# Keeping the feed-forward's steps in traced order on TensorE, in a kernel that adds an S4 convolution and a SiLU feed-forward

## The chip, the cores and the metric

The kernel runs on one core of a Trainium2 chip. The metric is the device time of one execution, in microseconds. A core has five engines with a queue each, which take their instructions in a fixed order: TensorE (PE, matrix products; its weight loads are shown as PEld), VectorE (DVE), ScalarE (ACT), GpSimd (POOL) and SyncE (SP, which here issues DMAs). They wait for each other through semaphores. Products land in PSUM, which the kernel divides into eight banks of 128 x 512 floats; the other operands lie in SBUF.

## The reference

```
xn  = layernorm(x)                       # x = A_u: 1 x 2048 x 576
K   = real(sum_n C * exp(dt*A*l) * dt*B)   # 576 x 2048, from 128 complex modes for each channel
y   = irfft(rfft(xn padded) * rfft(K padded))[:2048] + xn * Dskip
ffn = silu(xn @ w1) @ w2                 # w1: 576 x 4608, w2: 4608 x 576
out = x + y + ffn
```

`B_x` of the inputs is not used. All inputs and the output are float32.

## The kernel before

**Number format.** The large products run on operands split in two parts of a rounded float32 type, a high part `h` and a low part `l` (`h = round(v)`, `l = v - h`: a ScalarE copy and a VectorE subtraction). A product is then three matmuls into the same PSUM bank: h x h, h x l and l x h.

**The feed-forward, `ffn()`.** The 2048 tokens are 16 tiles (`j`) of 128. `half` is the first or second eight of them, `b` a group of four (512 tokens), and `c` one of nine chunks (`NCH`) of 512 of the 4608 hidden units, each of four tiles `t` of 128. A block is `(half, c, b)`: 36 blocks. There are two kinds of step, eight of them for each block:

- `up(blk, t)` (L320 to L342) makes 128 hidden units for 512 tokens: 12 matmuls of 512 columns at L331 (the three part products over four tiles of the contraction) and two at L332 and L333 for the last 64 input channels, all into one bank `ph` (pool `ps1`, two banks). ScalarE then applies the silu (`gf`) and rounds it (`gh`), and VectorE makes `gl`.
- `down(blk, jj)` (L344 to L365) multiplies the block's four `gh`/`gl` pairs with a chunk of w2 for one token tile: for each of two column halves (288 columns) 12 matmuls at L357 into one bank `po` (pool `ps2`, three banks), which VectorE then adds to the accumulator `acc[j]` (L361). In the last chunk of the second half `add_conv` goes ahead of it and adds the convolution's result.

The main loop traces, for block i, first `up` for t = 0 of block i + 1, then the four `down` steps of block i, then `up` for t = 1, 2, 3 of block i + 1; between them it loads and splits the next chunk's weights. The very first block is made ahead of the loop, in half-width pieces (256 tokens, `a` and `e` give the range), so that it can begin with the first two token tiles.

**The side stages, `side()`.** In order: `phase0` (load x, normalize, transpose tiles 0 to 7 into `xh`, `xl`, `x4`; `put_xt`, `put_x4`), the same for tiles 8 to 15 through DRAM (`late`), `natural` (the convolution's parameters), `kgen` (18 rounds, each with 64 small products `kp` at L696 and 8 products `z` at L711), `spread` (products `pu` at L161 and L162), `spectral` (products `pk`, `pu`, `pb` through `mm3`, L826), and `tail`, which with `add_conv` makes the last products `py` (L847). `weave` advances side stages and feed-forward together by given shares of the feed-forward's steps.

**What sets the order.** The Python code traces instructions; a scheduler then lays out each engine's list ahead of the run. It goes by priority, which is the traced order except where `tc.high_priority()` moves an instruction ahead, and it keeps its own account of when operands and buffers come free: where the instruction next in line would wait, another that is ready goes first. `behind(ins)` adds an edge: the instructions in its block stand behind `ins` in the list of their engine. It makes no semaphore wait of its own. `pins` holds instructions to point such edges at; `pins["pe"]` is the last matmul traced so far of an up or down step. Before the change, only two kinds of feed-forward matmuls have such an edge: the half-width ups for t = 2 and 3 of the first block, and in `add_conv` the first product.

Of the kernel before, what the change touches and what calls it, by code (L numbers as in the profile page):

```python
# [26 lines left out]
HD = D // 2  # L27
# [16 lines left out]
def kernel(  # L44
# [21 lines left out]
    nc = tc.nc  # L66
    FT = 4
# [72 lines left out]
    pins = {}  # L140

    def behind(ins):
        return tc.issue_after(ins) if ins is not None else nullcontext()
# [24 lines left out]
    def load_x(j, pool, tag, engines):  # L168

        t = pool.tile([P, 2, D], F32, tag=tag, name=f"{tag}{j}")  # L170
        for i in range(2 if j == 0 else 1):
            for ps, v, eng in quarters(xv, engines):
                if j:
                    eng.dma_start(t[ps], v[:, j:j + 2])
                else:
                    eng.dma_start(t[ps, i], v[:, i])
        pairs[j] = t
        return t[:, 0, :], t[:, 1, :]
# [78 lines left out]
    def ffn():  # L257
        w2v = w2.rearrange("(t p) d -> p t d", p=P)
        blocks = [(half, c, b) for half in range(2) for c in range(NCH) for b in range(2)]
        W1, W2, G = {}, {}, {}  # L260
# [60 lines left out]
        def up(blk, t, a=0, e=512, after=None):  # L321

            half, c, b = blk
            xh, xl, x4 = xts[2 * half + b]
            h1, l1 = W1[half, c, t]
            pool, tag = (ps2, "ps2") if e == 256 and t > 1 else (ps1, "ps1")
            ph = pool.tile([P, 512], F32, tag=tag, name="ph")[:, a:e]
            for n, (w, v) in enumerate(((h1, xh), (h1, xl), (l1, xh))):
                for kt in range(NKT):
                    with behind(after):  # L330
                        nc.tensor.matmul(ph, w[:, kt, :], v[:, kt, a:e], start=n + kt == 0, stop=False)  # L331
            nc.tensor.matmul(ph, h1[:, 4, :], x4[:, a:e], start=False, stop=False)  # L332
            pins["pe"] = nc.tensor.matmul(ph, l1[:, 4, :], x4[:, a:e], start=False, stop=True).ins  # L333
            gf = gp.tile([P, 512], F32, tag="gf", name="gf", bufs=2)[:, a:e]
            if a == 0:
                G[blk, t] = [gp.tile([P, 512], F32R, tag=n, name=n) for n in ("gh", "gl")]
            gh, gl = (g[:, a:e] for g in G[blk, t])
            with tc.high_priority():
                nc.scalar.activation(gf, ph, AF.Silu)  # L339
                pins["gh"] = nc.scalar.copy(gh, gf).ins  # L340
                with behind(pins["w1l2"] if e == 256 else None):
                    pins["gl"] = nc.vector.tensor_sub(gl, gf, gh).ins  # L342

        def down(blk, jj):  # L344
            half, c, b = blk
            j = 8 * half + 4 * b + jj
            js = slice(jj * P, (jj + 1) * P)
            if half == 1 and c == NCH - 1:
                if jj % 2 == 0:
                    add_conv(j, (acc[j], acc[j + 1]))  # L350
            for h in range(2):
                hs = slice(h * HD, (h + 1) * HD)
                po = ps2.tile([P, 512], F32, tag="ps2", name="po")
                n = 0
                for t in range(FT):
                    for g, w in ((0, 0), (0, 1), (1, 0)):
                        pins["pe"] = nc.tensor.matmul(po[:, :HD], G[blk, t][g][:, js], W2[half, c, t][w][:, hs],  # L357
                                                      start=n == 0, stop=n == 3 * FT - 1).ins
                        n += 1
                with tc.high_priority():  # L360
                    nc.vector.tensor_add(acc[j][:, hs], po[:, :HD], acc[j][:, hs])  # L361
            if half == 0 and c == NCH - 1:
                rows = slice(j * P, (j + 1) * P)
                nc.sync.dma_start(dr0[rows, :], acc[j])
                if j % 2:  # L365
                    acc[7 + j], acc[8 + j] = load_x(7 + j, accp, "acc", (nc.sync,))
# [34 lines left out]
        for t in range(FT):  # L401
            if t == 2:
                second = pins["pe"]
            up(blocks[0], t, 0, 256, second if t > 1 else None)
        for t in range(FT):
            up(blocks[0], t, 256, 512)
            yield 3.0

        for i, blk in enumerate(blocks):
            half, c, b = blk  # L410
# [3 lines left out]
            if half == 0 and c == NCH - 1:  # L414
                next_xt(b)

            after = {
                (0, "u0"): [(load_w1, 0)],
                (0, "u1"): [(split_w1, 0), (load_w2, 0), (load_w2, 1)],
                (0, "u2"): [(load_w1, 2)],  # L420
                (1, "u0"): [(split_w1, 2), (split_w2, 0), (load_w2, 2)],
                (1, "d3"): [(split_w2, 1), (load_w2, 3), (split_w2, 2)],
                (1, "u2"): [(split_w2, 3)],
            }
            if new == (1, NCH - 1):

                after = {
                    (0, "u0"): [(load_w1, 0), (load_w2, 0), (load_w2, 1), (load_w1, 2), (load_w2, 2), (load_w2, 3)],
                    (0, "u1"): [(split_w1, 0)],
                    (1, "u0"): [(split_w1, 2), (split_w2, 0)],  # L430
                    (1, "d3"): [(split_w2, 1), (split_w2, 2)],
                    (1, "u2"): [(split_w2, 3)],
                }
            for step in ("u0", "d0", "d1", "d2", "d3", "u1", "u2", "u3"):
                k = int(step[1])
                if step[0] == "d":
                    down(blk, k)
                    yield 3.0
                elif later:
                    up(blocks[i + 1], k)  # L440
                    yield 3.0
                for f, t in after.get((b, step), ()) if more else ():
                    f(*new, t)
                if half == 0 and c == NCH - 1:
                    for kt in {"d3": (0, 1), "u1": (2, 3), "u2": (4,)}.get(step, ()):
                        split_xt(b, kt)
# [391 lines left out]
    def add_conv(j, dsts):  # L838

        py = [pool.tile([P, 512], F32, tag=t, name="py") for pool, t in ((pss, "pss"),) * 3 + ((ps2, "ps2"),)]  # L840
        first = pins["pe"]
        for n in range(16):
            i, q1, q2, h = 1 - n // 8, n // 4 % 2, n // 2 % 2, 1 - n % 2
            o = 64 * q1 + 32 * q2
            rows = slice(64 * h, 64 * h + 64)
            with tc.high_priority() if n else nullcontext(), behind(first):
                mm = nc.tensor.matmul(py[2 * i + h][o:o + 32, :HD], s4[rows], yss[j + i][rows, 2 * q2 + q1],  # L847
                                      start=True, stop=True, tile_position=(64 * h, o), skip_group_check=True)
            if n == 0:
                first = mm.ins  # L850
        for i in range(2):
            del yss[j + i]
            for h in range(2):
                hs = slice(h * HD, (h + 1) * HD)
                nc.vector.tensor_add(dsts[i][:, hs], py[2 * i + h][:, :HD], dsts[i][:, hs])
        for _ in range(2):
            conv_load()
# [165 lines left out]
```

## Time and profile before

| What | us |
|---|---|
| Three runs | 1109.95, 1111.25, 1111.63 |
| Median | 1111.25 |
| Span of the profiled execution, first to last instruction | 1108.2 |
| TensorE matmuls busy | 1102.2 |
| Weight loads busy (beside the matmuls) | 997.5 |
| VectorE busy | 916.6 |
| ScalarE busy | 706.9 |
| GpSimd busy | 72.1 |

The profile has one row for each group of instructions: engine, line of the kernel, operation, what it writes and reads (buffer numbers left out), and how many. In a timeline the two first numbers are the start and the length in microseconds, and brackets give the time for which the engine sat idle ahead of the row and what released it. "Idle" ends when the last semaphore comes. The ends of matmuls are modelled, so that matmuls that follow each other closely overlap in the rows; their starts are recorded. The time of a run is some microseconds longer than the span of the profiled execution, which counts from the first instruction to the last.

The largest groups of DMA are the loads of w1 and w2, 512 and 288 KB each, the spectral stage's operands, and the stores and loads by which the convolution's data change their layout through DRAM.

### The profile page before, as it was taken

To read this page: it belongs to the slowest core of one execution; us is meant where nothing else is said; L and a number is where in the kernel's file an instruction comes from. 1 tells how busy PE (TensorE), PEld (TensorE's weight loads), DVE (VectorE), ACT (ScalarE), POOL (GpSimd) and SP (SyncE) were. 2 spreads that over 40 slices of the span, in tenths; PEclk is the share of its full clock that TensorE was granted. 3 is DMA by queue.
4 is the path that set the end of the run, shared out by engine and by line. 5 is a ranking of instruction groups with operands and counts; after the bars stand their busy time and mean duration, and the time that the engine had idled before them with its cause. 6 is when DMAs were issued, how large, how long until landed. Compare 5 with 4: busy or idle time off the path is not lost.

```text
span 1108.2 us, 22917 instructions
## 1 busy us (share of the span) xinstructions
PE 1102.2 (99%) x9167; PEld 997.5 (90%) x9167; DVE 916.6 (83%) x1543; ACT 706.9 (64%) x1222; POOL 72.1 (7%) x129
## 2 busy tenths in 40 slices
PE   9999999999999999999999999999999999999998
PEld 7989998899998899899999989999999999999887
DVE  7799899999999999999999737787778778784433
ACT  4564466676677676677867536877777878774210
POOL 1100000000000000011000000000000000000111
PEclk9999999999999999999999999999999999999999
DMA  9745512525252525264744173554544455434983
GB/s 270 190 123 160 152 50 61 120 73 131 77 121 83 116 72 118 77 174 154 206 122 103 45 179 109 162 167 123 156 145 152 138 149 170 129 107 127 241 224 87
DMA packets 175755, 148.56 MB, mean 134 GB/s; under 512 B 111088, under 2 KB 142592, under 8 KB 175520
## 3 DMA queue, kind: packets, MB, share of 16 engines
q1 hardware_dynamic: 165328, 112.63, 38.7%
q0 software_dynamic: 9568, 33.62, 9.6%
q8 instruction: 72, 1.18, 0.5%
q10 hardware_dynamic: 752, 0.85, 0.3%
q14 instruction: 35, 0.29, 0.1%
HBM read 102.53 MB, written 44.61 MB: 133 GB/s over the span
## 4 chain that ended last, share of the span: by engine, by line
PE 98%; DMA 1%; DVE 1%; SPq 0%; issue 0%; DVEq 0%
PE po L357 42%; PE ph L331 35%; PE kp L696 3%; PE ph L332 3%; PE ph L333 3%; PE pu L826 2%; PE pb L826 2%; PE pk L826 2%; PE z L711 2%; PE pu L161 1%; PE py L847 1%; DMA acc<-in_A_u_dram 1%; PE pu L162 1%; PE pt L124 0%; DVE w1l L295 0%; PE ptk L490 0%
## 5 line engine op out<-in xcount | busy, mean ns | idle before, releaser
L357 PE MATMUL po<-w2l,gh 128*128 128x288 f32 x1152 | 338.5, 295 | 0.0
L357 PE MATMUL po<-w2h,gl 128*128 128x288 f32 x1152 | 336.4, 295 | 0.0
L357 PE MATMUL po<-w2h,gh 128*128 128x288 f32 x1152 | 336.1, 295 | 0.0
L357 PEld LDWEIGHTS po<-w2h,gh 128*128 128x128 f32 x1152 | 215.2, 188 | 7.7 <-issue 2.8
L357 PEld LDWEIGHTS po<-w2l,gh 128*128 128x128 f32 x1152 | 215.9, 188 | 5.1 <-issue 0.5
L357 PEld LDWEIGHTS po<-w2h,gl 128*128 128x128 f32 x1152 | 215.4, 188 | 0.9
L339 ACT ACTIVATE gf<-ph 128x512 f32<-128x512 f32 (+1 forms) x148 | 86.4, 584 | 143.8 <-PE ph L333 134.8
L331 PE MATMUL ph<-xh,w1l 128*128 128x512 f32 (+1 forms) x592 | 161.3, 385 | 0.0
L331 PE MATMUL ph<-xh,w1h 128*128 128x512 f32 (+1 forms) x592 | 161.3, 387 | 0.0
L331 PE MATMUL ph<-xl,w1h 128*128 128x512 f32 (+1 forms) x592 | 161.1, 385 | 0.0
L361 DVE TENSOR_TENSOR acc<-po,acc 128x288 f32<-128x288 f32 x288 | 126.2, 451 | 37.0 <-PE po L357 35.6
L342 DVE TENSOR_TENSOR gl<-gf,gh 128x512 fp32r<-128x512 f32 (+1 forms) x148 | 99.0, 672 | 64.6 <-ACT gh L340 63.8
L331 PEld LDWEIGHTS ph<-xh,w1l 128*128 128x128 f32 x592 | 108.0, 188 | 20.0
L331 PEld LDWEIGHTS ph<-xl,w1h 128*128 128x128 f32 x592 | 107.9, 188 | 19.8
L331 PEld LDWEIGHTS ph<-xh,w1h 128*128 128x128 f32 x592 | 104.5, 188 | 16.7 <-ACT x L133 0.5
L340 ACT CAST gh<-gf 128x512 fp32r<-128x512 f32 (+1 forms) x148 | 89.5, 608 | 9.5 <-PE po L357 6.6
L653 ACT ACTIVATE c<-th,magic 128x1040 f32<-128x1040 f32 x36 | 42.1, 1168 | 37.9 <-DVE C L676 28.0
L655 ACT ACTIVATE c<-th 128x1040 f32<-128x1040 f32 x36 | 38.7, 1075 | 33.6 <-DVE th L654 33.6
L314 ACT CAST w2h<-w2r 128x576 fp32r<-128x576 f32 x72 | 47.0, 671 | 17.7 <-PE po L357 14.9
L295 DVE TENSOR_TENSOR w1l<-w1r,w1h 128x640 fp32r<-128x640 f32 x72 | 56.9, 817 | 0.2
L332 PE MATMUL ph<-x,w1h 128*128 128x512 f32 (+1 forms) x148 | 57.0, 386 | 0.0
L333 PE MATMUL ph<-x,w1l 128*128 128x512 f32 (+1 forms) x148 | 56.9, 385 | 0.0
(185 smaller groups left out, 1828.8 us busy)
## 6 DMA issues: line engine op xcount, KB each, us to landing
w2r<-in_B_w_dram SPq DMA_DIRECT2D x72, 288.0 KB, 3.8
w1r<-in_B_w_dram SPq DMA_DIRECT2D x35, 512.0 KB, 3.8
d1u<-u POOLq DMA_DIRECT2D x32, 288.0 KB, 2.5
d1k<-stage SPq DMA_DIRECT2D x18, 512.0 KB, 6.8
ur<-d1u SPq DMA_DIRECT2D x32, 288.0 KB, 3.7
kr<-d1k SPq DMA_DIRECT2D x32, 288.0 KB, 2.9
d<-yo POOLq DMA_DIRECT2D x32, 288.0 KB, 4.0
ys<-d SPq DMA_DIRECT2D x32, 288.0 KB, 11.8
```

What stands on the lines that cost most here:

```text
L295: pins["w1l"] = nc.vector.tensor_sub(l1, src, h1).ins
L314: pins["w2h"] = nc.scalar.copy(h2, r2).ins
L331: nc.tensor.matmul(ph, w[:, kt, :], v[:, kt, a:e], start=n + kt == 0, stop=False)
L332: nc.tensor.matmul(ph, h1[:, 4, :], x4[:, a:e], start=False, stop=False)
L333: pins["pe"] = nc.tensor.matmul(ph, l1[:, 4, :], x4[:, a:e], start=False, stop=True).ins
L339: nc.scalar.activation(gf, ph, AF.Silu)
L340: pins["gh"] = nc.scalar.copy(gh, gf).ins
L342: pins["gl"] = nc.vector.tensor_sub(gl, gf, gh).ins
L357: pins["pe"] = nc.tensor.matmul(po[:, :HD], G[blk, t][g][:, js], W2[half, c, t][w][:, hs], start=n == 0, stop=n == 3 * FT - 1).ins
L361: nc.vector.tensor_add(acc[j][:, hs], po[:, :HD], acc[j][:, hs])
L653: nc.scalar.activation(c65, th, AF.Identity, bias=magic)
L826: nc.tensor.matmul(dst, st, mv[:, hs], start=n == 0, stop=n == 3 * len(terms) - 1)
```

## The change

Each matmul of a down step gets an edge to the last feed-forward matmul traced ahead of that half step (`head`). In an up step of full width the twelve matmuls of L331 get one to the last feed-forward matmul traced ahead of the step (`after`). The half-width ups of the first block stay as they were. An instruction of a side stage has no such edge, and may stand between any two matmuls of the feed-forward. Nothing else is edited; lines behind the edits move by 2 or 4.

```
@@ up @@
             h1, l1 = W1[half, c, t]
             pool, tag = (ps2, "ps2") if e == 256 and t > 1 else (ps1, "ps1")
             ph = pool.tile([P, 512], F32, tag=tag, name="ph")[:, a:e]
+            if after is None and a == 0 and e == 512:
+                after = pins["pe"]
             for n, (w, v) in enumerate(((h1, xh), (h1, xl), (l1, xh))):
                 for kt in range(NKT):
                     with behind(after):
@@ down @@
             for h in range(2):
+                head = pins["pe"]
                 hs = slice(h * HD, (h + 1) * HD)
                 po = ps2.tile([P, 512], F32, tag="ps2", name="po")
                 n = 0
                 for t in range(FT):
                     for g, w in ((0, 0), (0, 1), (1, 0)):
-                        pins["pe"] = nc.tensor.matmul(po[:, :HD], G[blk, t][g][:, js], W2[half, c, t][w][:, hs],
-                                                      start=n == 0, stop=n == 3 * FT - 1).ins
+                        with behind(head):
+                            pins["pe"] = nc.tensor.matmul(po[:, :HD], G[blk, t][g][:, js], W2[half, c, t][w][:, hs],
+                                                          start=n == 0, stop=n == 3 * FT - 1).ins
                         n += 1
```

In the old list of TensorE the matmuls of up to three `po` and of one or two `ph` were interleaved; in the new one each `ph` and each `po` is finished before the next begins, with side products in between.

More of the change, by code (lines that the diff above doesn't have):

```diff
@@ L327, in up @@
             ph = pool.tile([P, 512], F32, tag=tag, name="ph")[:, a:e]
+            if after is None and a == 0 and e == 512:
+                after = pins["pe"]
             for n, (w, v) in enumerate(((h1, xh), (h1, xl), (l1, xh))):
@@ L351, in down @@
             for h in range(2):
+                head = pins["pe"]
                 hs = slice(h * HD, (h + 1) * HD)
@@ L356, in down @@
                     for g, w in ((0, 0), (0, 1), (1, 0)):
-                        pins["pe"] = nc.tensor.matmul(po[:, :HD], G[blk, t][g][:, js], W2[half, c, t][w][:, hs],
-                                                      start=n == 0, stop=n == 3 * FT - 1).ins
+                        with behind(head):
+                            pins["pe"] = nc.tensor.matmul(po[:, :HD], G[blk, t][g][:, js], W2[half, c, t][w][:, hs],
+                                                          start=n == 0, stop=n == 3 * FT - 1).ins
                         n += 1
```

## The prediction

> **What bounds the kernel now.** I read the page's totals first, then the chain of waits, then the timelines of the first 50 us, then the busy time by stage.
>
> ```profile
> span 1108.2 us, 22917 instructions
> PE 1102.2 (99%) x9167; PEld 997.5 (90%) x9167; DVE 916.6 (83%) x1543; ACT 706.9 (64%) x1222; POOL 72.1 (7%) x129
> PEclk9999999999999999999999999999999999999999
> PE 98%; DMA 1%; DVE 1%; SPq 0%; issue 0%; DVEq 0%
> ```
>
> TensorE is 99% of the span and 98% of the chain. Matmul ends are modelled, so "busy" alone could hide waits; the distance between starts can't. From the chain in order of time, and from a timeline in the middle of the kernel:
>
> ```profile
> 71.45 3.86 PE ph L331 x17
> 101.01 4.78 PE po L357 x36
> ...
> 301.19 0.62 PE L331 MATMUL ph<-xh,w1h 128*128 128x512 f32 x2
> 301.65 0.29 PE L357 MATMUL po<-w2h,gh 128*128 128x288 f32 x1
> ...
> 303.10 0.29 PE L357 MATMUL po<-w2h,gl 128*128 128x288 f32 x1
> 303.23 0.40 PE L331 MATMUL ph<-xh,w1h 128*128 128x512 f32 x1
> ```
>
> An up matmul (512 columns, L331) takes 3.86/17 = 0.227 us from start to start, a down matmul (288 columns, L357) 4.78/36 = 0.133 us. Going from up to down costs nothing (301.65 - 301.19 = 0.46 us for two ups), nor from down to up (303.23 - 303.10 = 0.13 us). TensorE is a full pipe, and the order in which the feed-forward's matmuls fill it has no price of its own. A new order can only lose, by making the pipe wait for an operand or a buffer, unless there are waits to win back. VectorE is the next candidate:
>
> ```profile
> 17.00:40.82 23.82, 23.67 (x189) 23.47 (x189) 21.89 (x59) 13.96 (x29) 3.87 (x4) 1.00 0.84 243
> 40.82:167.00 126.18, 126.18 (x740) 113.45 (x738) 113.95 (x192) 71.80 (x102) 4.81 (x5) 1.00 0.48 125
> 167.00:636.00 469.00, 469.00 (x4973) 423.32 (x4975) 451.84 (x677) 323.98 (x487) 21.52 (x39) 1.00 0.41 109
> 636.00:1050.00 414.00, 414.00 (x2727) 381.63 (x2716) 294.00 (x536) 281.55 (x578) 28.76 (x53) 1.00 0.53 149
> ```
>
> (Columns: stretch, length, then PE, PEld, DVE, ACT, POOL busy.) While the convolution kernel is built (167 to 636 us) VectorE is busy 451.84 of 469 us, so only 17.2 us are free; after 636 it has 29% free. Before 41 us, while x and the weights are being prepared, it is busy 92% too.
>
> **The change, part by part.** No matmul, copy or DMA is added or removed; the lists of instructions hold the same work. What moves:
>
> *1. The first block's down products go behind the second block's first up.* Compared instruction by instruction, TensorE's old list has all 96 down matmuls of block (0, 0, 0) ahead of block 1's first up product (token tiles 4 to 7). The new list has none of the 96 there: after the last half-width up of block 0 come the transposes of tiles 4 to 7, then that up, and only then the downs. In the old order the 96 downs were what TensorE did while those tiles were prepared:
>
> ```profile
> 28.98 0.64 PE L331 MATMUL ph<-xh,w1h 128*128 128x256 f32 x4
> 30.53 0.29 PE L333 MATMUL ph<-x,w1l 128*128 128x256 f32 x1
> 30.66 0.60 PE L124 MATMUL pt<-ident,xn 128*128 128x128 f32 x4
> 37.63 0.60 PE L124 MATMUL pt<-ident,xn 128*128 128x128 f32 x4
> 40.82 2.00 PE L331 MATMUL ph<-xh,w1h 128*128 128x512 f32 x8
> ```
>
> Block 1's first up began at 40.82. TensorE was full until then (23.67 of 23.82 us from 17 on), so without the 96 downs it would get there at 40.82 - 96 x 0.133 = 28.05. When are its operands there? They come from VectorE (xl, L126):
>
> ```profile
> 27.93 0.57 DVE L202 TENSOR_SCALAR xn<-acc,mv,sd 128x576 f32<-128x576 f32 x1
> 28.92 0.82 DVE L361 TENSOR_TENSOR acc<-po,acc 128x288 f32<-128x288 f32 x2
> 29.66 0.57 DVE L202 TENSOR_SCALAR xn<-acc,mv,sd 128x576 f32<-128x576 f32 x1
> 30.14 0.45 DVE L361 TENSOR_TENSOR acc<-po,acc 128x288 f32<-128x288 f32 x1
> 30.58 1.53 DVE L193 BATCH_NORM_STATS2 st<-xj 128x6 f32<-128x288 f32 x4
> 33.07 0.40 DVE L361 TENSOR_TENSOR acc<-po,acc 128x288 f32<-128x288 f32 x1
> 33.95 0.69 DVE L126 TENSOR_TENSOR xl<-pt,xh 128x512 fp32r<-128x512 f32 x1 [0.36 <-ACT xh L125]
> 36.10 0.58 DVE L202 TENSOR_SCALAR xj<-xj,mv,sd 128x576 f32<-128x576 f32 x1 [0.81 <-POOL sd L198]
> 36.91 0.82 DVE L361 TENSOR_TENSOR acc<-po,acc 128x288 f32<-128x288 f32 x2 [0.16 <-PE po L357]
> 38.91 0.76 DVE L250 STREAM_TRANSPOSE tr<-xj 128x576 f32<-128x576 f32 x1
> 39.60 0.65 DVE L126 TENSOR_TENSOR xl<-pt,xh 128x512 fp32r<-128x512 f32 x1
> 40.28 0.42 DVE L135 TENSOR_TENSOR x<-pt,x 64x256 fp32r<-64x256 f32 x1
> ```
>
> VectorE's list is unchanged up to the xn at 27.93. The last xl ended at 39.60 + 0.65 = 40.25. In the new list the six adds of L361 in this stretch stand behind it (0.82 + 0.45 + 0.40 + 0.82, less about 0.3 of overlap: 2.2 us), so does one tr (0.7), and the three waits (0.36 + 0.81 + 0.16 = 1.3) should go, since other work now stands between sd and its use and TensorE transposes earlier. 40.25 - 2.2 - 0.7 - 1.3 = 36.05. The up can do its first four matmuls (xh) ahead of that; ten more at 0.227 follow, so it ends at 38.3, where without the wait it would have ended at 28.05 + 14 x 0.227 = 31.2. **Loss: 7.1 us.** Above: if the three waits stay, 8.4. Below, ScalarE's own list:
>
> ```profile
> 26.48 0.79 ACT L339 ACTIVATE gf<-ph 128x256 f32<-128x256 f32 x2 [2.88 <-DVE gl L342]
> 28.66 0.87 ACT L207 ACTIVATE xn<-acc,mb,sd 128x576 f32<-128x576 f32 x1 [0.80 <-POOL sd L198]
> 31.29 0.59 ACT L125 CAST xh<-pt 128x512 fp32r<-128x512 f32 x1
> ```
>
> From 28.66 it has two xn (0.87), four xh (0.59), two copies of about 0.4 and the last silu and its rounding (0.8) to do: 28.66 + 1.74 + 2.36 + 0.8 + 0.8 = 34.4, then one xl of 0.65, 35.0: 6.1 us is the least. The row at 26.48 also shows that nothing is won ahead of this: block 0's last half up needs a buffer that this silu frees, so it can't start before about 26.9, and TensorE already stands there without the downs. What is queued behind the waiting up: all 96 downs and the first `ptk` transposes; who waits for those: VectorE's adds and the silu of block 1, both 7 us later against the work than now.
>
> [...]
>
> *2. From there to the first kernel product (kp, L696).* Counted along the lists, each instruction at its spacing in the trace, 124.9 us of TensorE work lie between that up and the first kp (before: 126.3), and VectorE has 111.7 us to do between its last piece of x (L135) and kp's tables (before: 112.3).
>
> ```profile
> 167.08 0.34 PE L696 MATMUL kp<-C 128*32 128x64 f32 x8
> ```
>
> Before, VectorE had 167.1 - 40.7 = 126.4 us for its part, 14.1 more than the work: waits and lead. Now it has (35.15 + 124.9) - 36.5 = 123.5 us, 11.8 more. If its waits stay as they were, TensorE waits 2.3 us at the first kp or at a po buffer ahead of it. One of these waits was on block 1's first up:
>
> ```profile
> 47.31 0.69 DVE L342 TENSOR_TENSOR gl<-gf,gh 128x512 fp32r<-128x512 f32 x1 [3.69 <-ACT gh L340]
> ```
>
> That one should shrink, since VectorE now comes to it with more behind it. So 0 to 2.3; I take **1.1 us**, the middle.
>
> *3. The kernel stage, 167 to 636 us.* By the lists the first kp stands 14.3 us of TensorE work earlier than before and the last at the same place, so the stage holds 14.3 us more TensorE work, and 3.7 us more of VectorE's: its free time grows from 17.2 to about 28 us. On average it is relieved. But each down step must now wait for its own buffer: `po` has three, so the add (L361) must be done two steps (3.2 us) after its step ended, and nothing else of the feed-forward may go in between. In the old lists, downs of three `po` were woven with ups. A kernel-stage operation of VectorE in front of an add is 1.2 us; once in each of the 18 rounds would be 21.6 us, never is 0. Walking the lists for adds that end late against an earlier add that VectorE itself had to wait for, I find three places, none above 2 us. I take **0.8 us**.
>
> *4. After 636 us, and the DMAs.* VectorE has 120 us free, and the last block's lists agree but for one matmul: 0. The same loads stand in SP's queue with a few neighbours exchanged; weights are loaded a chunk ahead, so this is hidden by some 25 us of TensorE work, and if it weren't it would cost one load's landing once:
>
> ```profile
> w2r<-in_B_w_dram SPq DMA_DIRECT2D x72, 288.0 KB, 3.8
> ```
>
> **Sum.** 1108.2 + 7.1 + 1.1 + 0.8 = 1117.2 us of span. The runs' median of 1111.25 lies 3.05 above the profiled span: 1120.2, so 1120.
>
> **The rivals.** *VectorE takes the bound in the kernel stage.* For it: 451.84 of 469 us busy, and a strict order leaves TensorE nothing else of the feed-forward to do when an add is late. Against it: the stage's free time grows by 10 us. Price 0 to 21.6; at half of the rounds 10.8: 1131. It decides from the point at which an add ends over 3.2 us after its step.
> *Half clock after the gap.* The trace shows a half-speed TensorE once, at the start, though the granted clock shows 9 (full) throughout:
>
> ```profile
> 4.67 1.72 PE L879 MATMUL pz<-zero 128*128 128x512 bf16 x4
> 7.06 1.89 PE L879 MATMUL pz<-zero 128*128 128x512 bf16 x8
> ```
>
> 0.43 us each, then 0.22. In part 1 TensorE mostly stands from 28.6 to 36, but broken by transposes and four matmuls. If it fell back for as long as here (some 12 matmuls, 0.21 us each): 2.5 us more, 1122.7. [...]
> *The change doesn't bite:* tiles 4 to 7 are ready when TensorE gets there, and the loss is under 2 us: 1112. Against it: VectorE would have to be done 6 us earlier, with xn itself only starting at 27.93.
> *Faster:* the strict order removes small gaps. In the stage of 469 us the counted work is 461; if half of these 8 us went and part 1 were hidden, 1107. Against it: the gaps I find are at kp and z, whose number stays. It decides if tiles 4 to 7 are there by about 28 us.
>
> **How the numbers follow.** Forecast 0.64, VectorE bound 0.16, half clock 0.09, no bite 0.07, faster 0.04. Below: 6.1, no second and third term, and 4 us of gaps won: +2.1, 1113. Above: 8.4 + 2.3 and a third of rival one's worst (7 us), nearly 18: 1128. That leaves out the faster case, most of "no bite" and the upper half of the first rival, under 2 in 10. This kernel's measurement tells 0.2% (2.2 us) from no change: faster 0.04, same 0.07, slower 0.89.
>
> **What would show it.** Right: block 1's first up starts between 34 and 36 us, with TensorE broken up from 28.6 on, VectorE's adds of block 0 all behind it, and the first kp near 160 us; from 636 us on each stage as long as now. Wrong: that up starting near 28 (part 1 hidden), rows of `po` waiting for L361 all through 167 to 636 (rival one), or 512-column starts 0.43 us apart near 37 us (half clock). A time under 1113 means that part 1 failed.

## The result, and the profile after

The changed kernel takes 1146.74 us (median of five runs, 1143.45 to 1146.89) against 1110.96 before: 35.8 us more, a ratio of 1.0318 [1.0306, 1.0331]. The prediction had 1120, at most 1128. The direction was right, the size was not.

From the changed kernel's page: the totals, the chain by engine, and the costliest group of TensorE with its idle time and what ended it.

```profile
span 1144.6 us, 22890 instructions
PE 1114.1 (97%) x9167; PEld 1002.7 (88%) x9167; DVE 918.6 (80%) x1543; ACT 707.7 (62%) x1222; POOL 70.3 (6%) x129
PE 69%; DVE 15%; ACT 3%; DMA 2%; issue 2%; SPq 0%; DVEq 0%; ACTq 0%
L361 PE MATMUL po<-w2h,gh 128*128 128x288 f32 x1152 | 344.1, 299 | 18.6 <-DVE acc L365 18.6
```

Same number of matmuls, the same busy time of VectorE (918.6 against 916.6). But the chain, 98% TensorE before, now has 15% of VectorE, and TensorE stands 18.6 us in front of down steps (L361) until an add (L365) has emptied a `po` bank. Before, TensorE had no such wait at all. Where the 36.4 us of span went is seen by cutting the trace at the same instructions as before: the end of block 1's first up and the first and last kernel product (`kp`). The rows of the kernel products, before and after, give the two last cuts (first and last start):

```profile
L696 PE MATMUL kp<-S x1152: 218/219/220, 167.2 to 637.2; 128*32 128x64 f32 x192
L700 PE MATMUL kp<-S x1152: 219/219/219, 172.4 to 673.4; 128*32 128x64 f32 x192
```

And the changed kernel's stretches, the last of them up to 0.4 us ahead of the last kernel product; columns as in the prediction, the last three being granted clock, DMA share and GB/s:

```profile
17.00:38.20 21.20, 16.87 (x106) 14.30 (x107) 20.56 (x56) 13.63 (x29) 3.81 (x4) 0.92 0.93 264
38.20:172.30 134.10, 125.59 (x749) 112.75 (x748) 110.56 (x188) 66.20 (x91) 3.18 (x5) 0.99 0.43 114
172.30:673.00 500.70, 489.66 (x5097) 439.78 (x5099) 459.61 (x683) 331.45 (x498) 21.54 (x39) 0.99 0.40 104
```

- **Start.** 7.1 us, as predicted (below).
- **38.2 to 172.3.** The prediction had the first kernel product near 160; it came at 172.3, 12.3 us later.
- **First to last kernel product.** 501.0 us, before 470.0. Of the 31.0 more, 14.3 are work that the new lists moved into the stage (50 up and 22 down matmuls, at 0.227 and 0.133 us), and 16.7 are lost.
- **Behind the last kernel product.** 471.2 us (1144.6 - 673.4), before 471.0 (1108.2 - 637.2), with the same feed-forward matmuls in it.

7.1 + 12.3 + 16.7 + 0.2 = 36.3, the whole difference but for 0.1.

**The start, row by row.** TensorE's timeline after the change:

```profile
26.95 0.75 PE L333 MATMUL ph<-xh,w1h 128*128 128x256 f32 x4 [2.02 <-ACT gf L341]
34.19 1.18 PE L333 MATMUL ph<-xh,w1h 128*128 128x512 f32 x4 [0.46 <-ACT xh L125]
35.84 1.20 PE L333 MATMUL ph<-xl,w1h 128*128 128x512 f32 x4 [0.48 <-DVE xl L126]
38.03 0.39 PE L335 MATMUL ph<-x,w1l 128*128 128x512 f32 x1
38.27 0.29 PE L361 MATMUL po<-w2h,gh 128*128 128x288 f32 x1
```

Block 1's first up starts at 34.19, waits for `xl` until 35.84, and ends at 38.27, where the first down of block 0 follows. Predicted: a start between 34 and 36, `xl` at 36.05, the end at 38.3.

**The stall at 50 us.** VectorE's timeline, and then TensorE's:

```profile
52.31 1.54 DVE L193 BATCH_NORM_STATS2 st<-xj 128x6 f32<-128x288 f32 x4 [3.90 <-DMA xj<-in_A_u_dram]
53.76 0.44 DVE L365 TENSOR_TENSOR acc<-po,acc 128x288 f32<-128x288 f32 x1
```

```profile
54.26 0.40 PE L361 MATMUL po<-w2h,gh 128*128 128x288 f32 x1 [3.65 <-DVE acc L365]
56.12 1.91 PE L333 MATMUL ph<-xh,w1h 128*128 128x512 f32 x4
60.76 1.07 PE L333 MATMUL ph<-xh,w1h 128*128 128x512 f32 x4
```

VectorE waits 3.90 us for a DMA (a tile of x), with an add behind it in its list; TensorE waits 3.65 us for the add. Then the up at 56.12 runs at half speed (1.91 us for four matmuls, 1.07 at 60.76).

**The same lateness, before and after.** This pair of places is the core of the result. VectorE and then TensorE, kernel before:

```profile
534.15 0.45 DVE L361 TENSOR_TENSOR acc<-po,acc 128x288 f32<-128x288 f32 x1
534.51 0.68 DVE L342 TENSOR_TENSOR gl<-gf,gh 128x512 fp32r<-128x512 f32 x1
...
536.32 1.23 DVE L637 TENSOR_TENSOR th<-vt,fT 128x1040 f32<-128x1040 f32 x1
537.47 0.82 DVE L295 TENSOR_TENSOR w1l<-w1r,w1h 128x640 fp32r<-128x640 f32 x1
...
539.94 1.28 DVE L382 TENSOR_TENSOR xl<-xl,xh 128x512 fp32r<-128x512 f32 x2
541.14 0.81 DVE L361 TENSOR_TENSOR acc<-po,acc 128x288 f32<-128x288 f32 x2
```

```profile
534.37 0.29 PE L357 MATMUL po<-w2h,gl 128*128 128x288 f32 x1
...
537.81 0.29 PE L357 MATMUL po<-w2h,gl 128*128 128x288 f32 x1
537.94 1.09 PE L331 MATMUL ph<-xh,w1h 128*128 128x512 f32 x4
...
541.15 1.07 PE L331 MATMUL ph<-xh,w1h 128*128 128x512 f32 x4
```

A down step ended at 534.37 + 0.29 = 534.66, its add began at 541.14: 6.5 us late, with side operations of VectorE in front of it. From 538.1 on all three `po` banks were full, and TensorE didn't notice: from 537.94 it made an up, and from 541.15 another. Now the kernel after, VectorE and then TensorE:

```profile
594.74 0.69 DVE L680 SCALAR_TENSOR_TENSOR S<-th,C 128x512 f32<-128x512 f32 x1
...
598.54 1.22 DVE L641 TENSOR_TENSOR th<-vt,fT 128x1040 f32<-128x1040 f32 x1
599.69 0.44 DVE L365 TENSOR_TENSOR acc<-po,acc 128x288 f32<-128x288 f32 x1
```

```profile
593.04 0.29 PE L361 MATMUL po<-w2h,gl 128*128 128x288 f32 x1
...
596.48 0.29 PE L361 MATMUL po<-w2h,gl 128*128 128x288 f32 x1
600.18 0.40 PE L361 MATMUL po<-w2h,gh 128*128 128x288 f32 x1 [3.41 <-DVE acc L365]
```

A down step ended at 593.33, its add began at 599.69: 6.4 us late, the same. Two further steps filled the other banks by 596.8. Next in TensorE's list is the fourth down step, the ups come behind it, and TensorE stands 3.41 us.

Over all adds whose step and start can be paired in the trace between 170 and 640 us (start of the add less end of the last matmul of its `po`), the mean is 2.87 us before (56 of 128 over 2.9 us) and 2.26 us after (34 of 119; to the end of its stage at 673 us, 2.12 us, 34 of 128). The pairing goes by order, and where steps are interleaved it takes as a step's last matmul the earliest that can be it, so single values of before may be too large. From 640 us to the end of the kernel before, the mean is 0.83 us. The adds were not made late by the change; they had been late all along.

### The profile page after: what moved, and what is told of

Same layout as the page of the kernel before. It is cut to its first block, busy times and chain, and to the rows that moved or that the text cites. A ratio compares the mean times of both kernels' runs of the same rounds, so it can differ in the third digit from the quotient of the medians.

```text
span 1144.6 us, 22890 instructions
## 1 busy us (share of the span) xinstructions
PE 1114.1 (97%) x9167; PEld 1002.7 (88%) x9167; DVE 918.6 (80%) x1543; ACT 707.7 (62%) x1222; POOL 70.3 (6%) x129
## 4 chain that ended last, share of the span: by engine, by line
PE 69%; DVE 15%; ACT 3%; DMA 2%; issue 2%; SPq 0%; DVEq 0%; ACTq 0%
PE po L361 30%; PE ph L333 24%; PE pu L830 2%; PE pb L830 2%; PE pk L830 2%; PE ph L335 2%; PE ph L334 2%; DVE C L668 2%; PE kp L700 2%; DMA w2r<-in_B_w_dram 2%; DVE gl L344 1%; DVE th L641 1%; DVE S L679 1%; DVE w1l L295 1%; DVE C L664 1%
## 5 line engine op out<-in xcount | busy, mean ns | idle before, releaser
L361 PE MATMUL po<-w2h,gh 128*128 128x288 f32 x1152 | 344.1, 299 | 18.6 <-DVE acc L365 18.6
L361 PE MATMUL po<-w2h,gl 128*128 128x288 f32 x1152 | 341.5, 296 | 0.5 <-DVE gl L344 0.5
L361 PE MATMUL po<-w2l,gh 128*128 128x288 f32 x1152 | 340.7, 296 | 0.0
L361 PEld LDWEIGHTS po<-w2h,gh 128*128 128x128 f32 x1152 | 217.4, 189 | 27.6 <-DVE acc L365 22.4
L361 PEld LDWEIGHTS po<-w2l,gh 128*128 128x128 f32 x1152 | 217.5, 189 | 1.5 <-DVE w2l L316 0.2
L361 PEld LDWEIGHTS po<-w2h,gl 128*128 128x128 f32 x1152 | 217.5, 189 | 1.4 <-DVE gl L344 1.1
L365 DVE TENSOR_TENSOR acc<-po,acc 128x288 f32<-128x288 f32 x288 | 127.4, 454 | 42.6 <-PE po L361 41.2
L333 PE MATMUL ph<-xh,w1l 128*128 128x512 f32 (+1 forms) x592 | 158.9, 386 | 0.0
L657 ACT ACTIVATE c<-th,magic 128x1040 f32<-128x1040 f32 x36 | 42.0, 1166 | 36.2 <-DVE C L680 19.6
L659 ACT ACTIVATE c<-th 128x1040 f32<-128x1040 f32 x36 | 38.7, 1074 | 36.4 <-DVE th L658 36.4
L316 DVE TENSOR_TENSOR w2l<-w2r,w2h 128x576 fp32r<-128x576 f32 x72 | 53.8, 755 | 6.1 <-ACT w2h L314 5.9
```

The source lines that it names most:

```text
L316: pins["w2l"] = nc.vector.tensor_sub(l2, r2, h2).ins
L657: nc.scalar.activation(c65, th, AF.Identity, bias=magic)
```

## The experiments

In the diffs, against the changed kernel, `i` stands for the block's number, `blk[0] * 2 * NCH + blk[1] * 2 + blk[2]`, 0 to 35. "Over before" is the difference of the medians of runs on the same chip; the last column is TensorE's wait for adds in the profile (`po` <- `acc`).

| Run | Edges | us | Ratio to before | Over before | Waits for adds |
|---|---|---|---|---|---|
| changed kernel | all | 1146.74 | 1.0318 [1.0306, 1.0331] | 35.8 | 18.6 |
| e1 | downs only | 1125.22 | 1.0129 [1.0114, 1.0144] | 14.4 | 0.3 |
| e2 | ups only | 1148.50 | 1.0341 [1.0326, 1.0357] | 37.7 | 20.0 |
| e3 | not in the first block | 1137.43 | 1.0235 [1.0217, 1.0252] | 26.6 | 16.7 |
| e4 | behind the kernel stage only | 1111.08 | 1.0002 [0.9992, 1.0012] | 0.4 | none |
| e5 | in the kernel stage only | 1135.82 | 1.0234 [1.0214, 1.0255] | 25.0 | 14.9 |
| e6 | all, late VectorE work behind adds | 1143.11 | 1.0290 [1.0275, 1.0305] | 32.2 | 8.8 |
| e7 | all, the tile of x behind an add | 1140.96 | 1.0278 [1.0257, 1.0299] | 30.1 | 13.4 |
| e8 | downs only, not in the first block | 1117.96 | 1.0065 [1.0048, 1.0082] | 7.1 | none |
| e9 | as e3, ups t = 1 to 3 free of the downs | 1117.18 | 1.0055 [1.0040, 1.0070] | 6.3 | none |
| e10 | as e3, up t = 1 free of the downs | 1130.65 | 1.0178 [1.0162, 1.0193] | 20.0 | 11.7 |
| e12 | as e3, four `po` banks | 1196.39 | 1.0770 [1.0754, 1.0786] | 85.7 | 2.7 |
| e13 | before, four `po` banks | 1184.62 | 1.0662 [1.0645, 1.0678] | 73.9 | none |

**Where: e3, e5 and e4.** The edges are taken away by block.

```
e3   if after is None and a == 0 and e == 512 and i > 1:
e3   head = pins["pe"] if i > 0 else None
e5   both with 4 < i < 23
e4   after: and i > 23;  head: if i > 22
```

> The edges are left off the first block's down steps and the second block's up steps; all others have them. Theory A (two losses that add: 7 us at the start, because the first 96 down products lie behind the second block's first up, and some 28 us later, because the adds that free the po banks stand late in VectorE's list): 1146.7 - 7 = 1139 to 1140, less 2 to 4 more if the half-clock stretch after the first wait goes with it, so 1135 to 1140. Theory B (the late start pushes VectorE behind and the later waits follow from it): 1111 to 1116.

> Edges only on blocks 5 to 22, which run while the convolution kernel is built (about 167 to 636 us). Theory A: the stage's own loss of some 17 us comes alone, 1126 to 1130. Theory B: without the late start nothing is late, 1111 to 1114. Theory C (both are needed, half each): about 1119.

> The change's edges only from the 24th block on, that is behind the kernel stage; the 23 blocks ahead of it are as before. Theory: the chained order costs only where VectorE is late with the adds, and behind the kernel stage it is not: 1109 to 1113 us, as before, and TensorE waits for no add. Rival (the chained order has a price everywhere, small in each block, e.g. when TensorE goes from one bank to the next): 13 of 36 blocks would cost at least 2 of the change's 36 us, more likely 5: 1113 to 1120.

Giving the first block its old order back wins 9.3 us (1146.74 to 1137.43), and the waits for adds stay (16.7 us). So the losses are two, and most of the second doesn't follow from the late start. e4 shows that the chained order has no price of its own: 13 of 36 blocks chained, 0.4 us, inside what can be measured. It costs where VectorE is late, and behind the kernel stage it hardly is (0.83 us in the mean). In the changed kernel, with every block chained, the work behind the last kernel product takes no longer either. e5 (1135.82) lies above its 1126 to 1130, and its 25.0 us above the 16.7 that the changed kernel lost in the stage. Its kernel products run from 165.4 to 663.4 us, with 9.3 us of feed-forward work moved in: 18.7 us are lost there. The rest, some 7.5 us, lies ahead of the stage, where block 5's ups are chained already.

**Which edges: e1, e2 and e8.**

```
e1   if after is None and a == 0 and e == 512 and False:
e2   head = None
e8   as e1, and head = pins["pe"] if i > 0 else None
```

> Only the down products have edges; the ups are free to go ahead. Theory A: the start's 7 us stay (the first down's head is the second block's first up). In the kernel stage TensorE can do an up while a po bank is not yet free, so that most of the 17 us go: 1120 to 1130. If it is the interleaving of three po banks that hid the late adds, and not the ups, the loss stays: 1140 to 1147.

> Only the full-width ups have edges; the down products are free, three banks at a time as before. Theory A: nothing is lost at the start (the downs may go ahead), and late adds are covered by other po banks' products as before: 1111 to 1116. If it is the ups' place that matters (TensorE has no up to fill a wait with): 1125 to 1140.

> Edges on down products only, and not on the first block's. If the start's loss and the ups' edges are separate terms: 1125.2 - 7 to 9 = 1116 to 1118. If the start's loss was hiding a wait of the same size: 1122 to 1125.

I had looked for the second loss at the downs, each waiting for its bank, and expected e2 near the time before. It lies above both ranges and is as slow as the full change (1148.50), without the start's loss; why its later loss is the larger is open. And e1, with the downs chained and the ups free, has no waits for adds (0.3 us). It is the **ups'** edge that makes TensorE wait for adds. e8 lands where e1 less the first block's loss should (1125.22 less some 7): the start is a loss by itself. The 7.1 us that e8 still costs hold no wait for an add.

**Is it VectorE's order? e6 and e7.** In e6, the kernel stage's later VectorE and ScalarE work (from L657 to the tables' L680) gets an edge to the add traced last; in e7, only the normalization of the tiles of x that come late.

```
e6, e7  pins["add"] = nc.vector.tensor_add(acc[j][:, hs], po[:, :HD], acc[j][:, hs]).ins
e6      with behind(pins["add"]):      # around the body from L657 to L680
e7      with behind(pins["xn" if j == 8 else "gl"]), behind(None if j == 8 else pins["add"]):
```

> As the changed kernel, and each round of the kernel stage has its VectorE and ScalarE work kept behind the last add (L365) traced so far. Theory P (place: TensorE waits because the scheduler put kernel-stage work in front of adds whose products were already there): TensorE's waits for the adds, 18.6 us, fall below 6, and the time to 1122 to 1135, not lower, since VectorE now waits for TensorE at the adds. Theory T (throughput: VectorE is simply full in this stage, and the wait shows up wherever it is put): 1144 to 1155.

> As the changed kernel, and the normalization of tiles 10 to 15 is kept behind the last add traced so far, so that the row statistics of tile 10, which wait 3.90 us for their load, no longer stand ahead of an add. Theory P: the 3.8 us stall near 50 us and the half-clock stretch behind it (1.6 us) go, and perhaps the 1.7 us stall near 80: 1139 to 1142. Theory T: the time comes back later, 1145 to 1148.

e7 came as expected (1140.96): the stall at 50 us and the half speed behind it are gone. e6 (1143.11) missed its 1122 to 1135 and lies just under the 1144 to 1155 of the rival. From its list of waits, TensorE's row and VectorE's:

```profile
PE po L361 <- DVE acc L365: 8.8, 10, 3.8
DVE acc L365 <- PE po L361: 66.2, 69, 3.3
```

TensorE's wait for adds is halved, but an edge can't make an add early: VectorE now stands 66.2 us waiting for `po` (41.2 in the changed kernel) and then has its own work behind. Pushing VectorE's work back moves the wait more than it removes it.

**What TensorE did meanwhile: e9 and e10.** If the adds were as late before, TensorE must have had other work; in the feed-forward that can only be ups, which are independent of `po`. Both start from e3.

```
e9   if after is None and a == 0 and e == 512 and i > 1 and t != 1:
e10  as e9, and the ups with t == 2 also behind the last matmul of the last down:
     with behind(after), behind(pins["down"] if after is not None and t == 2 and i > 1 else None):
```

> As the run without the first block's edges (1137.4), with one of the four ups of each block (t = 1) free to go ahead. Theory F (an up is what TensorE does while an add is late; one up of 3.2 us for each block is enough): 1116 to 1126. If all ups must be free: 1130 to 1138.

> As e3 and e9 (the first block as before, downs chained), but here only the up with t = 1 is free to go between the downs; those with t = 2 and 3 stand behind the last down. In e9 the ups with t = 2 and 3 had followed the free one: their edge pointed at it and no longer at the downs, so e9 had up to three ups to put between the downs. Theory F1 (one up as something to do is enough): 1115 to 1121, TensorE waits under 4 us for adds. Theory F3 (TensorE needs several of them, since VectorE falls behind more than once in the eight half steps of a block): 1124 to 1132, waits for adds 6 to 12 us.

e9 came as expected for a wrong reason: the edge of the up with t = 2 points at the up with t = 1, so freeing that one freed all three of the downs. e10 frees one alone, and its waits for adds are 11.7 us:

```profile
PE po L361 <- DVE acc L366: 11.7, 10, 2.6
```

One up in each block wins 6.7 of e3's 26.6 us, the next two another 13.7, and 6.3 stay. One up in eight half steps isn't enough to cover the late adds. In e9 the adds are even later than before (3.03 us in the mean of 170 to 640 us, counted as above), and TensorE never waits for one.

**A fourth bank: e12 and e13.**

```
ps2: bufs=3 -> 4, pss: bufs=3 -> 2
py = [... ((pss, "pss"),) * 2 + ((ps2, "ps2"),) * 2]
```

> As e3 (chained ups and downs, the first block as before), with four po banks in place of three; the side stages have two banks in place of three. If TensorE stands because a po bank is not free when the fourth step comes, a fourth bank lets an add be 1.6 us later (one half step): waits for adds fall from 16.7 to under 6 us and the time from 1137 to 1121 to 1129, plus what the bank is worth to the side stages (the run e13 shows that). If the banks are not what it waits for, the time stays at 1137 or above.

> The kernel before, with four po banks and two for the side stages: what the lost side bank costs by itself. TensorE was full without it: 1110 to 1118. If the side stages need the third bank (kp and z alternate in them), more.

The side bank that had to go is worth 74 us to the kernel before, far above the 1118 that I allowed, so that as a version this is out. Only 7 of the 74 us fall up to the last kernel product (644.4 us in e13, 637.2 before); the rest lies behind it. So the experiment still answers its question: with a fourth bank the chained order waits 2.7 us for adds, not 16.7, and costs 11.8 us over the same kernel without edges (1196.39 - 1184.62), not 26.6. The last kernel product is 12.0 us later (656.4 against 644.4). Most of what stays isn't the adds: e12's list has 10.7 us of waits of up and down steps for `gf`, `gh` and `gl`.

## Why the prediction was right or wrong

**Part 1, the first block: right, and in size.** Loss 7.1 us predicted; the up ends at 38.27 where 38.3 was forecast. e8 against e1 gives 7.3. With the ups chained it is 9.3 (e3), which takes in a stall further on.

**Part 2, up to the first kernel product: 1.1 us predicted, 12.3 measured.** The sum compared VectorE's work with the time it had, and took its waits as they were. One of them, on a tile of x, had an add behind it, and TensorE had nothing in front of the next down step but that add: 3.65 us, and half speed afterwards (1.6 us; e7 wins 5.8 in all). Five shorter waits for adds, of the same kind as in part 3, make 4.5 us more; some 2.5 us were not broken down.

**Part 3, the kernel stage: 0.8 us predicted, 16.7 measured. This is the step that failed.** "Walking the lists for adds that end late against an earlier add that VectorE itself had to wait for, I find three places, none above 2 us": this took VectorE to be in step with TensorE at such an add and never far behind in between. In the trace after, the latest add of the stage starts 6.6 us behind its step, and TensorE waits for adds eight times, 10.4 us in all. Half clock behind two of these waits costs another 3.2 (below); 3 us were not broken down. Why the walk found so little is open. The trace of before contradicts it, and it was there to be read: the adds' mean lateness of 2.87 us, next to the 3.2 us that the prediction itself named as the point from which it decides; by the same pairing 49 of 128 adds start later than that. I didn't look for them because TensorE never waited for an add, and took that as a sign that none was late. It was a sign that ups covered them. The argument against the rival, that the stage's free time grows by 10 us, was about averages: in the kernel after, VectorE is busy 459.61 of the stage's 500.70 us, has 41 us free, and is late at the places that matter.

**Part 4: right.** 471.2 us behind the last kernel product against 471.0, and e4.

**The rivals.** "VectorE takes the bound in the kernel stage", 0 to 21.6 us, was not a rival to the forecast but a part of it: 16.7. It was given 0.16, and half its price. "Half clock after the gap", priced at 2.5 us, came too, four times; from the windows of the changed kernel (TensorE's busy time and granted clock):

```profile
24.90:26.95 2.05, 0.03 (x1) 1.00 1.01 368
26.95:28.40 1.45, 1.45 (x12) 1.00 1.09 238
28.40:31.70 3.30, 2.87 (x15) 0.51 1.10 311
...
55.50:59.00 3.50, 3.50 (x12) 0.54 0.00 0
...
438.06:441.47 3.41, 3.07 (x13) 0.50 1.26 224
533.63:537.04 3.41, 3.41 (x16) 0.50 0.24 91
```

(1 - 0.51) x 3.30 = 1.6 us, (1 - 0.54) x 3.50 = 1.6 us, and half of the busy 3.07 and 3.41 us, 1.5 and 1.7. The first stood in time in which TensorE was waiting for tiles anyway, and part 1's sum held without it; the other three came on top. The range failed because forecast and rivals were treated as alternatives to choose from, where the late adds and the half clock add to the first block's loss. (Its upper end is also added up 1 us short: 1111.25 + 8.4 + 2.3 + 7 is 1129.)

**What is shown and what isn't.** Shown: the ups' edges are the costly ones (e1, e2), the cover is the ups behind the downs (e9, e10), a bank more does most of the same (e12), and behind the kernel stage nothing is lost (e4). Not fully broken down: the 7.1 us that stay in e8 and the 6.3 in e9, where TensorE's list of waits holds 6.6 us (1.7 before), in short waits for `xn`, `gf`, `gl` and others and none for an add; and why e2 loses more than the changed kernel behind the start. No version here is faster than the kernel before, whose TensorE is busy for 1102.2 of 1108.2 us.

## What to carry to other kernels

An engine that shows no wait for a buffer hasn't shown that the buffer is emptied in time; it may have had other work. Before an order is fixed, pair each producer with its consumer in the trace, compare the lateness with the slack that the buffers give, and name the work that fills the difference: if the new order puts that work behind the waiting instruction, the whole difference becomes a stall (here 3.41 us before 600.18, for an add that began 6.4 us late). Chain only steps that no engine needs as something to do, and measure the lateness in each stage, since the mean load of the late engine doesn't tell it.

## What the runs showed of the hardware

The granted clock didn't fall by the length of the last gap alone. After a gap of 2.02 us (up to 26.95) TensorE ran 1.45 us at full clock (1.00) and then 3.30 us at half (0.51); after the one of 3.65 us before 54.26 it fell too (0.54 from 55.50 to 59.00); after the 3.41 us before 600.18 it did not (first row below). Around the waits of 1.72 and 1.76 us before 438.40 and 532.77 it fell (0.50, last two rows above); around the 1.61 us before 380.74 it did not (last row):

```profile
596.00:600.50 4.50, 1.09 (x8) 1.00 0.17 66
377.00:385.00 8.00, 6.39 (x45) 1.00 0.98 213
```

Each fall lasted 3.41 us, at a granted clock of 0.50 (28.46 to 31.87, 55.77 to 59.18, 438.06 to 441.47 and 533.63 to 537.04). In the 3.41 us ahead of the four falls TensorE was busy for 1.50, 1.51, 1.92 and 1.65 us by the windows, but stretches of the same length with 1.67 to 1.82 us (from 48.94, 79.66, 595.08 and 598.49) were followed by none. So neither number tells the falls from the rest: the clock fell around a wait of 1.72 us and not after one of 3.41, and behind 1.92 busy us and not behind 1.67. What makes it fall was not shown.
